# Seven products for the third group's first layer, and decays of keys and states moved from GpSimd to ScalarE

## The chip, the cores and the metric

The kernel runs on one core of a Trainium2 chip. The metric is the device time of one launch in microseconds. TensorE is called PE, VectorE DVE, ScalarE ACT, GpSimd POOL and SyncE SP, as in the profile.

## The reference

Decayed linear attention (4 batches, 8 heads, 768 positions, head size 64, in blocks) is followed by a two-layer network over all 3072 tokens:

```python
for b in range(nb):
    intra = np.einsum('bhic,bhjc->bhij', qb, kb) * Dmask[None]
    intra = np.einsum('bhij,bhjd->bhid', intra, vb)
    inter = np.einsum('bhid,bhde->bhie', qb * lam_pow[None], kv_state)
    out[:, :, sl] = intra + inter
    kb_dec = kb * rev_pow[None]
    kv_state = lam_block[None, :, None, None] * kv_state + np.einsum('bhsd,bhse->bhde', kb_dec, vb)
...
h = x @ w_in                      # 512 -> 2048
sp = np.where(h > 20.0, h, np.log1p(np.exp(np.minimum(h, 20.0))))
g = h * np.tanh(sp)
return (g @ w_out).astype(np.float32)   # 2048 -> 512
```

All decays are powers of one number per head. So within a group of positions a key is scaled by a factor that depends on its position and head, and a state by one factor per head.

## The kernel before, in words

The 768 positions are cut into six groups of 128; a group holds 512 tokens, 128 of each batch. The groups are numbered 0 to 5 in the code, so that "the third group" is `n = 2`. For each group and batch:

- `load_pair` (L84) issues the loads of keys, queries and values from POOL, two batches at a time, with a cast to 16 bits. Each kind has four buffers.
- Keys and queries are transposed ("turned") either by PE and a copy (`turn_pe`, L221) or by SP's transposing DMA (`turn_dma`, L239), which writes `kT` and `qT` for two batches.
- `decay_k` (L246) multiplies keys by `lk`, giving `kd`, on DVE or POOL.
- `scores` (L250) multiplies `kT` with `qT` on PE; DVE masks the two halves.
- `outputs` (L272) adds the part from the state `w` and the part from the masked scores on PE; DVE scales the result to `xn`, and SP's transposing DMA (or PE and ACT) writes it to `xt`, the network's input.
- `state` (L299) multiplies `kd` with the values on PE; DVE adds the old state (`raw`), and `raw` times the table `lbm` gives the new state `w`, on POOL mostly.

The network's first layer takes `xt` of a group to `hsg`. Done plainly it is 16 units of four 128x512 matmuls (`unit`, L337). Done "by seven products" (`set_step`, L419) it works on 2x2 blocks: four sets (`set_of`), each with seven products of four 128x256 matmuls where eight would be needed. This takes sums of the weights (`w_sum`, four for each of four sets) and of the input (`x_sums`, four per group), both on DVE, two copies per set on ACT (`seed` and `p5`) and two additions on DVE (L437, L441). The second layer (`dense2`, L529) works by seven products for all groups but the first; it is cut into 14 halves, which the code calls with `h()` between the other work.

The order is written out by hand: each engine executes its instructions in the order in which the code names them, and waits at each until its operands are there. In the part from L812 on, the loop over `n` runs a stage in which group `n` has its second layer, `n + 1` its first, and `m = n + 2` its attention. The table `KINDS` says for each stage whether the first layer is plain (`p`) or by seven products (`s`); stage 1, which has the third group's first layer, is plain. Ahead of the loop, the second group's first layer runs by pairs of units (`two_units`), with the third group's attention between them, and then the first group's plain second layer (`plain2`).

POOL has one queue as well. Loads, decays of keys and decays of states stand in it in the order of the code. A load waits for its buffer, and for the landing of the load eight places before it.

Of the kernel before, what the change touches and what calls it, by code (L numbers as in the profile page):

```python
# [20 lines left out]
def kernel(  # L21
# [12 lines left out]
    C = 128  # L34
# [165 lines left out]
    def state_decays():  # L200
        lbt = lb.rearrange("p (j t) -> p t j", t=2)
        for hp in range(2):
            rs = slice(64 * hp, 64 * hp + 64)
            nc.vector.tensor_copy(lbm[rs, :, rs], bc(lbt[rs, hp, :], 2, D))

# [40 lines left out]
    def decay_k(n, b, eng):  # L246
        kd[n, b] = work.tile([128, H, D], F16, name="kd", tag="kd", bufs=4)
        eng.tensor_tensor(out=kd[n, b], in0=kn[n, b], in1=bc(lk, 2, D), op=ALU.mult)

    def scores(n, b, tags="eo"):  # L250
        p_ = [bank(t, [JP, C]) for t in tags]
        for j in range(JP):
            for t in range(2):
                rs = slice(64 * t, 64 * t + 64)
                nc.tensor.matmul(p_[t][:, j, :], kT[n, b][rs, j, :], qT[n, b][rs, j, :],  # L255
                                 start=True, stop=True)
        for t in range(2):
            tag, bufs = ("sb", 4) if n > 0 or b < 2 else (f"xsum{b % 2 * 2 + t}", 1)
            sb[n, b, t] = work.tile([128, JP, C], F16, name="sb", tag=tag, bufs=bufs)
            nc.vector.tensor_tensor(out=sb[n, b, t], in0=p_[t], in1=dm[:, t], op=ALU.mult)  # L260

# [10 lines left out]
    def outputs(n, b, turn=None, tag="z"):  # L272
# [11 lines left out]
        nc.vector.tensor_tensor(out=xn, in0=po, in1=bc(lq, 2, D), op=ALU.mult)  # L284
        dst = x_tile(n)[:, :, b * C : (b + 1) * C]
# [13 lines left out]
    def state(n, b, tag, eng, later=False, home=("raw", 2)):  # L299
# [8 lines left out]
        else:  # L308
            raw = work.tile([128, JP, 128], F32, name="raw", tag=home[0], bufs=home[1])
            nc.vector.tensor_tensor(out=raw, in0=pv, in1=wst[n, b], op=ALU.add)  # L310
            wst[n + 1, b] = w_new
            decay = lambda: eng.tensor_tensor(out=w_new, in0=raw, in1=lbm, op=ALU.mult)  # L312
            return decay if later else decay()
        wst[n + 1, b] = w_new
# [320 lines left out]
    scores(0, 0)  # L635
    turn_pe(0, 1, first_banks)
# [10 lines left out]
    for b in range(B):  # L647
        decay_k(0, b, nc.vector)
# [12 lines left out]
    state(0, 0, "e", nc.vector)  # L661
    state(0, 1, "o", nc.vector)
    unit(0, 2, "A")
    unit(0, 3, "B")
    state(0, 2, "e", nc.vector)
    state(0, 3, "o", nc.vector)
# [18 lines left out]
    def out1(b, turn, po, pv):  # L685
        later[b] = outputs(1, b, turn, po)
        return state(1, b, pv, nc.vector if b < 2 else nc.gpsimd, b < 2,
                     ("raw", 2) if b < 2 else (("p5", "c22")[b - 2], 1))
# [6 lines left out]
    for t in "kqv":  # L695
        load_pair(t, 2, 1)
    mask_decays()
    first_units(9, 10, 11, 4, 5, 6)
    decay_k(1, 0, nc.vector)
    turn1(0, "Hz")  # L700
    first_units(7)
    turn1(1, "GC")
    scores(1, 0)
    decay_k(1, 1, nc.vector)
# [13 lines left out]
    decay_k(1, 2, nc.vector)  # L718
# [12 lines left out]
    two_units(1, 8, 0)  # L731
# [3 lines left out]
    decay_k(2, 0, nc.vector)  # L735
    decay_k(2, 1, nc.vector)
    w_sum(0, 0, nc.vector)
    w_sum(0, 1, nc.vector)
    two_units(1, 12, 0)
    turn_dma(2, 1)  # L740

# [3 lines left out]
    def attended(n, b):  # L745
        outputs(n, b)
        state(n, b, "H", nc.gpsimd)
# [4 lines left out]
    w_sum(0, 2, nc.vector)  # L752
    w_sum(0, 3, nc.vector)
# [6 lines left out]
    two_units(1, 6, 1)  # L760
    weight_sum(0, 1)
    two_units(1, 8, 1)
    attended(2, 1)
    for t, bp in (("k", 0), ("q", 0), ("v", 0)):
        load_pair(t, 3, bp)
# [5 lines left out]
    w_sum(2, 0, nc.vector)  # L771
    w_sum(2, 1, nc.vector)
    w_sum(2, 2, nc.vector)
    w_sum(2, 3, nc.vector)
# [9 lines left out]
    decay_k(2, 2, nc.vector)  # L784
# [4 lines left out]
    decay_k(2, 3, nc.vector)  # L789
    weight_sum(2, 0)  # L790
    plain2(1, 2, 3)
    plain2(2, 0)
    attended(2, 3)
    for t, bp in (("k", 1), ("q", 1), ("v", 1)):
        load_pair(t, 3, bp)
    sums(1, 0, 0, 1)
    plain2(2, 1, 2, 3)
    weight_sum(2, 1)
    plain2(3, 0, 1, 2, 3)
    sums(1, 0, 2, 3)  # L800
    busy(1)
# [10 lines left out]
    KINDS = {1: "pppp", 2: "ssss", 3: "ssss", 4: "ssss"}  # L812
    WSUMS = {(1, 0): (1,), (1, 1): (3,)}

    for n in range(1, NG - 1):
# [3 lines left out]
        def u(*units):  # L819
            for ni in units:  # L820
                unit(n + 1, ni, next_bank())

        held = []

        def s_(b):
            if m < NG:
                if b == 0 and not last:
                    decay_k(m, 0, nc.gpsimd)
                scores(m, b)
                release()  # L830

        def o_(b):
            if m < NG:
                outputs(m, b)
                if last:
                    return
                if b < B - 1:
                    decay_k(m, b + 1, nc.gpsimd)
                if "s" in KINDS[n]:
                    held.append(lambda: state(m, b, "z", nc.gpsimd))  # L840
                else:
                    state(m, b, "e", nc.gpsimd)
# [10 lines left out]
        def ws(n, i):  # L853
            for x in WSUMS.get((n, i), ()):
                for t in range(4):
                    w_sum(x, t, nc.vector)

        kinds = KINDS[n]
        sets = []
        for i, x in enumerate((0, 2, 1, 3)):  # L860
            spare = ("e", "z", "o") if m >= NG else ("A", "C", "B")
            alone = (("A", "B", "C"), spare)
            turn = i % 2 if kinds[i - 1] == "s" else 0
            sets.append(set_of(n + 1, x, alone[turn]) if kinds[i] == "s" else None)
# [10 lines left out]
        def opening(i):  # L875

            if kinds[i] == "s":
                mm(i, "m1")
                s_(i)
                mm(i, "seed")  # L880
                if i != 1:
                    settle()
            elif i == 0:
                s_(i)
# [42 lines left out]
        fresh = kinds[0] == "s" and KINDS[n - 1][3] == "p"  # L927
# [3 lines left out]
        if "s" in kinds:  # L931
            x_sums(n + 1, 0, 1, 2, 3)
        if not fresh:
            opening(0)
        if m < NG:
            turn_dma(m, 1)
        if kinds[0] == "s":
            h(1)
            if fresh:
                mm(0, "m2")  # L940
                h(1)
                mm(0, "m5", "m6")
            else:
                mm(0, "m2", "m5", "m6")
                sums(n, 1, 0, 1)
                h(1)
            o_(0)
            fetch(("k", 0), ("q", 0))
            if fresh:
                h(1)  # L950
            closing(0)
        else:
            u(0)
            sums(n, 1, 0, 1)
            if n == 1:
                weight_sum(3, 0)
                weight_sum(3, 1)
            h(1)
            u(1)
            h(1)  # L960
            u(2)
            o_(0)
            fetch(("k", 0), ("q", 0))
            u(3)
# [5 lines left out]
        if kinds[1] == "s":  # L970
            settle()
            mm(1, "m2")
            h(1)
            mm(1, "m5", "m6")
            sums(n, 1, 2)
            h(1)
            o_(1)
            fetch(("v", 0), ("k", 1))
            closing(1)
        else:  # L980
            u(8)
            settle()
            s_(1)
            sums(n, 1, 2, 3)
            ws(n, 0)
            h(1)
            u(9, 10)
            o_(1)
            fetch(("v", 0), ("k", 1))
            h(1)  # L990
            u(11)
# [3 lines left out]
        if kinds[1] == "s":  # L995
            sums(n, 1, 3)
# [3 lines left out]
        if kinds[2] == "s":  # L1000
            mm(2, "m2", "m5", "m6")
            o_(2)
            fetch(("q", 1), ("v", 1))
            h(1)
            closing(2)
            h(1)
            sums(n + 1, 0, 0, 1)
            h(1)
        else:
            u(4)  # L1010
            settle()
            s_(2)
            u(5)
            ws(n, 1)
            h(1)
            u(6)
            o_(2)
            fetch(("q", 1), ("v", 1))
            h(1)
            sums(n + 1, 0, 0, 1)  # L1020
            h(1)
            u(7)
# [3 lines left out]
        if kinds[3] == "s":  # L1026
            h(1)
            mm(3, "m2", "m5")
            h(1)
            mm(3, "m6")  # L1030
            o_(3)
            h(1)
            mm(3, "m7", "m3")
            owed.append(3)
            release()
            sums(n + 1, 0, 2, 3)
        else:
            s_(3)
            h(1)
            u(12)  # L1040
            settle()
            h(1)
            o_(3)
            u(13)
            sums(n + 1, 0, 2, 3)
            h(1)
            u(14)
        more = n + 1 < NG - 1
        if more:
            halves = dense2(n + 1)  # L1050
            h(1)
        if kinds[3] == "s":
            if more:
                h(1)
            settle()
        else:
            settle()
            u(15)
            if more:
                h(1)  # L1060
# [33 lines left out]
```

## Time and profile before

| | |
|---|---|
| median of 3 runs | 204.99 us (204.48 to 205.32) |
| the profiled execution | 204.73 us |
| its span, first to last instruction | 202.9 us |
| PE busy | 194.7 us, 96% |
| DVE busy | 148.0 us, 73% |
| ACT busy | 98.2 us, 48% |
| POOL busy | 81.8 us, 40% |
| mean granted clock of PE | 0.994 |

A row of a timeline has the start and the length in us, the engine, the line of the code, the operation and its tiles (out<-in), and in brackets the idle time ahead of it and what ended that. `x4` means that four instructions are merged; matmuls are pipelined, so one lasts longer than the time to the next. The rows of DMA queues have packets, megabytes and the time of those packets as a share of 16 engines; q0 carries the loads that POOL issues, q1 what SP issues.

### The profile page before, as it was taken

The page shows a single profiled execution, that of the slowest core. Times are in us where ns is not written, and L with a number is a line of the kernel's source. Part 1 is how long each engine was busy: PE and PEld are TensorE (multiplying, and loading weights), DVE is VectorE, ACT ScalarE, POOL GpSimd, SP SyncE. Part 2 cuts the span into 40 slices and gives each one's busy share as a digit, 9 for nine tenths or more (in the row PEclk, how much of TensorE's full clock was granted, in tenths as well). Part 3 has the DMA queues.
Part 4 walks back from the last instruction along what each step waited for, and adds up shares of the span by engine and source line. Part 5 has one row for each costly group of instructions (what it writes and reads, how often), then busy time and mean ns, then how long its engine had stood idle before and what let it go on. Part 6 is the DMA issues. An engine that isn't in the chain of part 4 may idle for free.

```text
span 202.9 us, 4669 instructions
## 1 busy us (share of the span) xinstructions
PE 194.7 (96%) x1931; PEld 150.1 (74%) x1931; DVE 148.0 (73%) x247; ACT 98.2 (48%) x176; POOL 81.8 (40%) x78
## 2 busy tenths in 40 slices
PE   7989999989999999999999999999999999999990
PEld 3867456878855556667668888988888988888890
DVE  6597558699978977689868698699588657179041
ACT  4685664658431124342264672456465384826300
POOL 7999452580292590848493377230000000000020
PEclk9999999999999999999999999999999999999997
DMA  9999999999999999999999999983213211003123
GB/s 131 134 142 198 175 180 156 157 204 201 148 142 153 223 164 175 178 109 117 176 218 172 126 79 158 189 193 89 29 26 81 79 53 53 0 3 119 43 100 105
DMA packets 109336, 26.26 MB, mean 129 GB/s; under 512 B 99458, under 2 KB 108802, under 8 KB 109314
## 3 DMA queue, kind: packets, MB, share of 16 engines
q0 software_dynamic: 77568, 13.37, 91.3%
q1 hardware_dynamic: 30704, 12.33, 29.2%
q10 hardware_dynamic: 1042, 0.26, 0.6%
q8 instruction: 15, 0.25, 0.5%
q14 instruction: 7, 0.06, 0.1%
HBM read 27.26 MB, written 6.29 MB: 165 GB/s over the span
## 4 chain that ended last, share of the span: by engine, by line
PE 77%; DMA 9%; POOL 7%; ACT 2%; DVE 2%; issue 1%; POOLq 0%; DVEq 0%; ACTq 0%
PE bG L523 15%; PE bH L523 13%; DMA vn<-in_v_dram 8%; PE bB L412 6%; PE bC L412 5%; PE bA L412 4%; PE bA L329 3%; PE be L255 3%; PE bB L329 3%; PE bA L355 2%; PE bC L355 2%; PE bB L355 2%; POOL win L96 2%; PE bC L329 2%; PE bz L281 2%; PE bA L574 2%
## 5 line engine op out<-in xcount | busy, mean ns | idle before, releaser
L312 POOL TENSOR_TENSOR w<-raw,lbm 128x512 f16<-128x512 f32 x14 | 20.4, 1458 | 41.9 <-DVE raw L310 41.8
L523 PEld LDWEIGHTS <-gsum 128*128 128x128 f16 x336 | 31.2, 98 | 4.2
L523 PEld LDWEIGHTS <-hsg 128*128 128x128 f16 x240 | 23.0, 98 | 4.4
L605 POOL TENSOR_TENSOR c<-p,u 128x512 f32<-128x512 f32 x1 | 1.3, 1276 | 58.7 <-DVE p L604 58.7
L260 DVE TENSOR_TENSOR sb<-be,dm 128x512 f16<-128x512 f32 x22 | 15.1, 687 | 8.4 <-PE bo L255 8.4
L523 PE MATMUL bH<-tsum,gsum 128*128 128x256 f16 x160 | 20.4, 273 | 0.0
L329 PEld LDWEIGHTS <-win 128*128 128x128 f16 x136 | 12.6, 98 | 10.3 <-DMA win<-in_moe_w_in_dram 0.5
L412 PEld LDWEIGHTS <-wsum 128*128 128x128 f16 x192 | 18.5, 98 | 2.2
L523 PE MATMUL bG<-wout,hsg 128*128 128x256 f16 x160 | 19.9, 273 | 0.0
L486 DVE TENSOR_TENSOR gsum<-hsg 128x1024 f16<-128x1024 f16 x20 | 15.6, 784 | 1.6 <-ACT hsg L335 1.6
L412 PEld LDWEIGHTS <-win 128*128 128x128 f16 x144 | 13.8, 98 | 2.2 <-issue 0.5
L260 DVE TENSOR_TENSOR sb<-bo,dm 128x512 f16<-128x512 f32 x22 | 15.0, 680 | 0.0
L284 DVE TENSOR_TENSOR xn<-bz,lq 128x512 f16<-128x512 f32 x18 | 12.3, 685 | 2.9 <-PE bz L281 2.9
L355 PEld LDWEIGHTS <-win 128*128 128x128 f16 x128 | 12.0, 98 | 1.6
L87 POOL DMA_DIRECT2D kn<-in_k_dram x10 | 11.9, 1190 | 2.8 <-PE bB L329 1.5
L87 POOL DMA_DIRECT2D qn<-in_q_dram x10 | 11.8, 1179 | 1.7 <-PE bA L329 0.9
L87 POOL DMA_DIRECT2D vn<-in_v_dram x10 | 11.7, 1172 | 1.4 <-DMA win<-in_moe_w_in_dram 1.2
L416 ACT ACTIVATE hsg<-bC 128x512 f16<-128x512 f32 x10 | 5.9, 594 | 13.0 <-PE bC L412 13.0
L412 PE MATMUL bA<-xt,win 128*128 128x256 f16 x80 | 12.0, 272 | 0.1
L329 PE MATMUL bA<-xt,win 128*128 128x512 f16 x44 | 11.3, 380 | 0.0
L574 PEld LDWEIGHTS <-hsg 128*128 128x128 f16 x64 | 6.0, 98 | 6.9
L335 ACT ACTIVATE hsg<-bA 128x512 f16<-128x512 f32 x11 | 6.6, 597 | 8.6 <-PE bA L329 8.6
(189 smaller groups left out, 445.4 us busy)
## 6 DMA issues: line engine op xcount, KB each, us to landing
out_dram<-osum SPq DMA_DIRECT2D x23, 256.0 KB, 3.2
kn<-in_k_dram POOLq DMA_DIRECT2D x10, 256.0 KB, 8.7
qn<-in_q_dram POOLq DMA_DIRECT2D x10, 256.0 KB, 8.0
vn<-in_v_dram POOLq DMA_DIRECT2D x10, 256.0 KB, 9.7
wout<-in_moe_w_out_dram POOLq DMA_DIRECT2D x4, 512.0 KB, 15.2
win<-in_moe_w_in_dram POOLq DMA_DIRECT2D x3, 512.0 KB, 10.5
vz<-in_v_dram POOLq DMA_DIRECT2D x2, 256.0 KB, 6.5
kn<-in_k_dram POOLq DMA_DIRECT2D x3, 128.0 KB, 4.6
```

The source lines that it names most:

```text
L87: nc.gpsimd.dma_start(out=tile_, in_=rows(src, n, 2 * bp, 2))
L255: nc.tensor.matmul(p_[t][:, j, :], kT[n, b][rs, j, :], qT[n, b][rs, j, :], start=True, stop=True)
L260: nc.vector.tensor_tensor(out=sb[n, b, t], in0=p_[t], in1=dm[:, t], op=ALU.mult)
L284: nc.vector.tensor_tensor(out=xn, in0=po, in1=bc(lq, 2, D), op=ALU.mult)
L312: decay = lambda: eng.tensor_tensor(out=w_new, in0=raw, in1=lbm, op=ALU.mult)
L329: nc.tensor.matmul(open_[n, ni][:, lo:hi], win[ni // 4][:, kc, (ni % 4) * 128 : (ni % 4) * 128 + 128], xt[n][:, kc, lo:hi], start=(opens a ...
L335: nc.scalar.activation(h_tile(n)[:, ni, :], open_.pop((n, ni)), AF.Mish)
L355: nc.tensor.matmul(t[:, u, :], win[ni // 4][:, kc, m : m + 128], xt[n][:, kc, cs], start=(u == 0 and kc == 0), stop=(kc == NKC - 1), skip_ ...
L412: nc.tensor.matmul(t[:, u, :], lhs, rhs, start=(fresh and u == 0 and kk == 0), stop=(kk == 1), skip_group_check=True)
L486: nc.vector.tensor_tensor(out=gsum[n, i][:, ks, :], in0=a, in1=b, op=op)
L523: nc.tensor.matmul(t, lhs(kk, blk), rhs(kk)[:, lo:hi], start=(fresh and kk == 0), stop=(kk == HK - 1), skip_group_check=True)
L574: nc.tensor.matmul(po, hsg[n][:, ki, b * C : (b + 1) * C], wout[part][:, kk, :], start=(ki == 0), stop=(ki == NKI - 1))
```

## The change

The third group's first layer is done by seven products as the later ones are: stage 1 takes the branch that stages 2 to 4 took, and the code for plain stages is removed. It needs the weight sums earlier. Those of sets 0 and 2 now stand in the first group, that of set 1 in the second group's first layer, that of set 3 before its end, and the last sums of the second layer's weights before stage 1.

Keys of the third group's second pair and of the later groups are decayed by ACT, one head of two batches at a time (`decay_heads`, 128x128 each). States are added on DVE in two pieces, only the blocks that count, into two lasting tiles `raws` that are zeroed once, and are decayed by ACT with a scale per pair of heads, four instructions for a state (`decay` in `state`). POOL keeps two state decays of the second group. In the second group, the fourth batch's keys are decayed earlier, and the third batch's `xn` comes between the two halves of the fourth batch's score mask. The loads of the fourth group's second pair are named with the first pair's.

```diff
+    def decay_heads(m, pair=None):
+        if pair:
+            decayed_pair(*pair)
+            heads_left.extend(pair + (h,) for h in range(H))
+        for _ in range(min(m, len(heads_left))):
+            n, bp, h = heads_left.pop(0)
+            src, dst = pairs["k", n, bp], decayed[n, bp]
+            nc.scalar.activation(dst[:, h : 2 * H : H, :], src[:, h : 2 * H : H, :], AF.Copy,
+                                 scale=lk[:, h : h + 1])
...
-            nc.vector.tensor_tensor(out=raw, in0=pv, in1=wst[n, b], op=ALU.add)
-            wst[n + 1, b] = w_new
-            decay = lambda: eng.tensor_tensor(out=w_new, in0=raw, in1=lbm, op=ALU.mult)
-            return decay if later else decay()
+        raw = raws[b % 2]
+        for rs in (slice(0, 64), slice(64, 128)):
+            nc.vector.tensor_tensor(out=raw[rs, :, rs], in0=pv[rs, :, rs],
+                                    in1=wst[n, b][rs, :, rs], op=ALU.add)
+
+        def decay():
+            for j in range(JP):
+                nc.scalar.activation(w_new[:, j, :], raw[:, j, :], AF.Copy,
+                                     scale=lbp[:, j : j + 1])
+
+        return decay
...
     scores(1, 2)
+    decay_k(1, 3)
     two_units(1, 2, 0)
     two_units(1, 4, 0)
-    scores(1, 3)
-    out1(2, "G", "z", "H")
-    decay_k(1, 3, nc.vector)
+    mask3 = scores(1, 3, apart=True)
+    out1(2, "G", "z", "H", mask3)
     two_units(1, 6, 0)
     later[2]()
-    out1(3, "G", "e", "o")
     for decay in decays1:
         decay()
+    out1(3, "G", "e", "o")
...
     attended(2, 1)
-    for t, bp in (("k", 0), ("q", 0), ("v", 0)):
-        load_pair(t, 3, bp)
+    for bp in range(2):
+        for t in "kqv":
+            load_pair(t, 3, bp)
...
-    KINDS = {1: "pppp", 2: "ssss", 3: "ssss", 4: "ssss"}
-    WSUMS = {(1, 0): (1,), (1, 1): (3,)}
+    decays = []
...
+        def scaled(i):
+            while decays:
+                decays.pop(0)()
+            if i < 2:
+                if not last:
+                    decay_heads(H // 2, (m, 1) if i == 0 else None)
+            elif m + 1 < NG - 1:
+                decay_heads(H // 2, (m + 1, 0) if i == 2 else None)
...
+            mm(1, "m5")
+            scaled(1)
+            mm(1, "m6")
```

POOL's queue after the loads of the third group's second pair (`kn_461` and its two neighbours; numbers tell buffers apart, L87 are loads, L312 state decays, L248 key decays), before:

```order
L87 DMA kn_461<-in_k_dram 128x16x64
L87 DMA qn_463<-in_q_dram 128x16x64
L87 DMA vn_465<-in_v_dram 128x16x64
L312 TENSOR_TENSOR w2_436<-raw_757,lbm_134 128x512
L312 TENSOR_TENSOR w3_443<-raw_798,lbm_134 128x512
L312 TENSOR_TENSOR w0_410<-raw_943,lbm_134 128x512
L312 TENSOR_TENSOR w1_417<-raw_1013,lbm_134 128x512
L87 DMA kn_1016<-in_k_dram 128x16x64
L87 DMA qn_1018<-in_q_dram 128x16x64
L87 DMA vn_1020<-in_v_dram 128x16x64
L312 TENSOR_TENSOR w2_436<-raw_1124,lbm_134 128x512
L312 TENSOR_TENSOR w3_443<-raw_1185,lbm_134 128x512
```

The same place of POOL's queue in the changed kernel (L348 is the state decay that is left):

```order
L87 DMA kn_466<-in_k_dram 128x16x64
L87 DMA qn_468<-in_q_dram 128x16x64
L87 DMA vn_470<-in_v_dram 128x16x64
L348 TENSOR_TENSOR w2_441<-raw_770,lbm_134 128x512
L348 TENSOR_TENSOR w3_448<-raw_817,lbm_134 128x512
L87 DMA kn_1034<-in_k_dram 128x16x64
L87 DMA qn_1036<-in_q_dram 128x16x64
L87 DMA vn_1038<-in_v_dram 128x16x64
L87 DMA kn_1040<-in_k_dram 128x16x64
L87 DMA qn_1042<-in_q_dram 128x16x64
L87 DMA vn_1044<-in_v_dram 128x16x64
L87 DMA kn_1397<-in_k_dram 128x16x64
```

The decays of the third group's states (`w0_410<-raw_943` and on) no longer stand ahead of the fourth group's loads; its six loads and the fifth group's follow directly.

ACT's queue in the changed kernel, in the second set of the third group's first layer (L480 is the copy `p5`, L357 the state decays, L270 the key decays, L462 the activation, L472 the copy `seed`):

```order
L480 ACTIVATE p5_1472<-bB_1467 128x512
L357 ACTIVATE w0_415<-raw_152,lbp_154 128x128 x4
L270 ACTIVATE kd_1370<-kn_1040,lk_149 128x2x64 x4
L462 ACTIVATE hsg_1350<-bB_1467 128x2x256
L472 ACTIVATE bB_1554<-bA_1528 128x512
L462 ACTIVATE hsg_1350<-c22_1521 128x2x256
```

Eight small activations now stand between `p5` and the activation of the set's third result.

DVE's queue around the third and fourth batch of the second group in the changed kernel (L258 keys, L284 score masks, L313 `xn`, L347 and L352 states):

```order
L258 TENSOR_TENSOR kd_688<-kn_119,lk_149 128x512
L284 TENSOR_TENSOR sb_746<-be_736,dm_148 128x512
L313 TENSOR_TENSOR xn_761<-bz_748,lq_150 128x512
L284 TENSOR_TENSOR sb_763<-bo_737,dm_148 128x512
L347 TENSOR_TENSOR raw_770<-bH_765,w2_441 128x512
L313 TENSOR_TENSOR xn_810<-be_797,lq_150 128x512
```

Before, both masks stood ahead of the first `xn`, and this `kd` between the first `raw` and the second `xn`.

More of the change, by code (lines that the diff above doesn't have):

```diff
@@ L244, in turn_dma, with decayed_pair, decay_k, scores @@
                 to[n, 2 * bp + i] = tile_[:, i * JP : (i + 1) * JP, :]
[L246 to L250, printed above, removed]
+    decayed = {}
+    def decayed_pair(n, bp):
+        t = work.tile([128, 2 * H, D], F16, name="kd", tag="kd", bufs=2)
+        decayed[n, bp] = t
+        for i in range(2):
+            kd[n, 2 * bp + i] = t[:, i * H : (i + 1) * H, :]
+    def decay_k(n, b):
+        if b % 2 == 0:
+            decayed_pair(n, b // 2)
+        nc.vector.tensor_tensor(out=kd[n, b], in0=kn[n, b], in1=bc(lk, 2, D), op=ALU.mult)
+    heads_left = []
+    def decay_heads(m, pair=None):
[7 more added lines that the diff above has]
+                                 scale=lk[:, h : h + 1])
+    def scores(n, b, tags="eo", apart=False):
         p_ = [bank(t, [JP, C]) for t in tags]
@@ L256, in scores, with mask @@
                                  start=True, stop=True)
-        for t in range(2):
+        def mask(t):
             tag, bufs = ("sb", 4) if n > 0 or b < 2 else (f"xsum{b % 2 * 2 + t}", 1)
@@ L260, in scores @@
             nc.vector.tensor_tensor(out=sb[n, b, t], in0=p_[t], in1=dm[:, t], op=ALU.mult)
+        mask(0)
+        if apart:
+            return lambda: mask(1)
+        mask(1)
     def first_outputs(b, tag):
@@ L297, in outputs, with state @@
         return later
-    def state(n, b, tag, eng, later=False, home=("raw", 2)):
+    raws = [work.tile([128, JP, 128], F32, name="raw", tag="raw", bufs=2) for _ in range(2)]
+    lbp = const.tile([128, JP], F32, name="lbp")
+    def state(n, b, tag, home=None):
         pv = bank(tag, [JP, 128])
@@ L635 @@
     scores(0, 0)
+    for t in raws:
+        nc.vector.memset(t, 0.0)
     turn_pe(0, 1, first_banks)
@@ L683, in turn1, with out1 @@
         turn_pe(1, b, banks, "q", eng)
[L685 to L688, printed above, removed]
+    def out1(b, turn, po, pv, then=None):
+        later[b] = outputs(1, b, turn, po, then)
+        return state(1, b, pv, ("p5", "c22")[b - 2] if b > 1 else None)
     first_units(8)
@@ L817 @@
         last = m >= NG - 1
-        def u(*units):
-            for ni in units:
-                unit(n + 1, ni, next_bank())
         held = []
         def s_(b):
[L826 to L830, printed above, removed]
-        def o_(b):
[L833 to L842, printed above, removed]
+            scores(m, b)
+            release()
+        def o_(b):
+            outputs(m, b)
+            if not last:
+                held.append(lambda: decays.append(state(m, b, "z")))
+        def scaled(i):
+            while decays:
+                decays.pop(0)()
+            if i < 2:
+                if not last:
+                    decay_heads(H // 2, (m, 1) if i == 0 else None)
+            elif m + 1 < NG - 1:
+                decay_heads(H // 2, (m + 1, 0) if i == 2 else None)
         def release():
@@ L861 @@
             spare = ("e", "z", "o") if m >= NG else ("A", "C", "B")
-            alone = (("A", "B", "C"), spare)
-            turn = i % 2 if kinds[i - 1] == "s" else 0
-            sets.append(set_of(n + 1, x, alone[turn]) if kinds[i] == "s" else None)
+            sets.append(set_of(n + 1, x, (("A", "B", "C"), spare)[i % 2]))
         owed = []
@@ L999 @@
             turn_dma(m + 1, 0)
[L1000 to L1022, printed above, removed]
-        opening(3)
[L1026 to L1060, printed above, removed]
+        mm(2, "m2", "m5")
+        scaled(2)
+        mm(2, "m6")
+        o_(2)
+        fetch(("q", 1), ("v", 1))
+        h(1)
+        closing(2)
+        h(1)
+        sums(n + 1, 0, 0, 1)
+        h(1)
+        opening(3)
+        h(1)
+        mm(3, "m2", "m5")
+        scaled(3)
+        h(1)
+        mm(3, "m6")
+        o_(3)
+        h(1)
+        mm(3, "m7", "m3")
+        owed.append(3)
+        release()
+        sums(n + 1, 0, 2, 3)
+        halves = dense2(n + 1)
+        h(2)
+        settle()
     sums(NG - 1, 1, 2, 0, 1, 3)
```

167 lines of the change are left out of this document (74 added, 93 removed).

## Prediction

> **What bounds the kernel now.** I read the page's head first, then the engines' busy time in stretches, then the timelines of single engines around the places that the change touches.
>
> ```profile
> span 202.9 us, 4669 instructions
> PE 194.7 (96%) x1931; PEld 150.1 (74%) x1931; DVE 148.0 (73%) x247; ACT 98.2 (48%) x176; POOL 81.8 (40%) x78
> ```
>
> The reader should see one engine, TensorE (PE), at 96%. That is an average, so the stretches come next: the stage that holds the third group's first layer (73.30 to 105.57), and the one after it, which has seven products already.
>
> ```profile
> 73.30:105.57 32.27, 32.27 (x290) 22.06 (x288) 24.43 (x40) 12.52 (x21) 20.06 (x17) 1.00 1.81 159
> 105.57:134.55 28.98, 28.98 (x323) 25.21 (x320) 24.08 (x39) 14.53 (x27) 14.46 (x13) 1.00 1.41 153
> ```
>
> The columns are length, then busy time of PE, weight loads, DVE, ACT and POOL. PE is busy for the whole of both at full clock. So a matmul less there is time gained, and work added to VectorE (DVE) or ScalarE (ACT) costs nothing until it makes PE wait. The only waits of PE between 32 and 134 us stand here, in its timeline:
>
> ```profile
> 41.80 0.40 PE L293 MATMUL bG<-ident,xn 128*128 128x128 f16 x4 [0.32 <-DVE xn L284]
> ...
> 42.99 0.40 PE L302 MATMUL bo<-vn,kd 128*128 128x128 f16 x4 [0.34 <-DVE kd L248]
> ```
>
> **The matmuls.** 64 matmuls of 128x512 go, 112 of 128x256 come (16 units of four; 4 sets of seven products of four). Their spacing, from the same timeline:
>
> ```profile
> 84.43 1.03 PE L329 MATMUL bC<-xt,win 128*128 128x512 f16 x4
> 85.29 1.03 PE L329 MATMUL bA<-xt,win 128*128 128x512 f16 x4
> ...
> 110.89 0.60 PE L412 MATMUL bB<-xsum,wsum 128*128 128x256 f16 x4
> 111.33 0.60 PE L412 MATMUL bC<-xt,wsum 128*128 128x256 f16 x4
> 111.76 0.60 PE L412 MATMUL bA<-xt,win 128*128 128x256 f16 x4
> ```
>
> Four of 512 take 85.29 - 84.43 = 0.86 us; four of 256 take (111.76 - 110.89)/2 = 0.435. So 16 x 0.86 = 13.76 becomes 28 x 0.435 = 12.18: **1.58 us less**. A check: the first stretch holds 16 eighths-of-a-second-layer, the second 14, each eight matmuls of 256 (0.87); 32.27 - 28.98 - 2 x 0.87 = 1.55.
>
> What pays for it: the extra input sums and the eight extra combining adds go to DVE, whose load becomes about that of the second stretch (24.08 of 28.98, under which PE lost nothing), and weight sums go earlier. Nothing on the path.
>
> **The stall at 41 to 43 us.** The change computes the fourth batch's decayed keys earlier, and puts DVE's `xn` ahead of the second half of the score mask. Each of the two waits above is shorter than the one DVE operation taken out from in front of it, so I take both as gone: **0.66 us less**. Bounds: 0, if the eight new ACT decays queued there delay the next group's `qT` as long; and 0.66.
>
> **ACT's small decays.** 8 per pair of batches for keys and 4 per state are added, none of which the trace shows. Nearest rows: a 128x8 with a scale read from memory, and the 128x512 around the place where the decays will sit, behind `p`:
>
> ```profile
> 11.85 0.30 ACT L191 ACTIVATE lk<-lnb,ek 128x8 f32<-128x8 f32 x1
> 12.04 0.30 ACT L191 ACTIVATE lq<-lnb,eq 128x8 f32<-128x8 f32 x1
> ...
> 108.84 0.60 ACT L545 ACTIVATE osum<-bG 128x512 f32<-128x512 f32 x1 [0.28 <-PE bG L523]
> 109.36 0.60 ACT L434 ACTIVATE p<-bC 128x512 f32<-128x512 f32 x1
> 111.96 0.60 ACT L416 ACTIVATE hsg<-bC 128x512 f16<-128x512 f32 x1 [2.01 <-PE bC L412]
> ```
>
> Spacing 0.19 at 8 elements and 0.52 at 512 bound one of 128 elements; in proportion it is 0.19 + 0.33 x 120/504 = 0.27, which I take. The largest batch, eight, is 2.2 us, against an idle 2.01 in that very place. A spill of 0.2 us delays the activations behind it, and PE only where a bank comes free late. I cost it at nothing. Without cover (0.52 each, 4.2 us) five such places would lose up to 2 us each.
> [...]
>
> **GpSimd's queue (POOL), which I take to decide.** POOL issues every load, in order, between its own multiplications:
>
> ```profile
> 42.42 3.44 POOL L312 TENSOR_TENSOR w<-raw,lbm 128x512 f16<-128x512 f32 x2 [0.16 <-DVE raw L310]
> 52.04 1.27 POOL L312 TENSOR_TENSOR w<-raw,lbm 128x512 f16<-128x512 f32 x1 [6.18 <-DVE raw L310]
> 55.78 1.65 POOL L312 TENSOR_TENSOR w<-raw,lbm 128x512 f16<-128x512 f32 x1 [2.47 <-DVE raw L310]
> 57.37 1.21 POOL L87 DMA_DIRECT2D kn<-in_k_dram  x1
> ```
>
> The fourth group's loads start at 57.37 only because POOL sat behind the states at 52.04 and 55.78. Those two multiplications leave POOL. Its row after the pair at 42.42 is now the load, so loads start near 45.9 us, 11.5 us sooner, and six stand in one run, with the fifth group's behind. POOL's freed time is worth nothing in itself; what it triggers is. At that moment SP turns the third group's second pair (`kT`, `qT`) by DMA:
>
> ```profile
> SPq L242 <- DMA kn<-in_k_dram: 55.5, 2, 53.1
> ```
> ```profile
> 54.33 1.32 SPq L242 DMA_TRANSPOSE kT<-kn  x1
> 55.77 1.25 SPq L242 DMA_TRANSPOSE qT<-qn  x1
> ```
>
> SP waited for the load of `kn` until 54.33. That load is in the opening stream and does not move with PE, so these turns keep their start. Time from issue to landing, from the DMA view around each `qT` turn: first this one, then those issued at 66.84, 91.72, 105.43 and 121.00, each with loads under way:
>
> ```profile
> qT<-qn SPq DMA_TRANSPOSE x1, 3.4
> ```
> ```profile
> qT<-qn SPq DMA_TRANSPOSE x1, 4.5
> ```
> ```profile
> qT<-qn SPq DMA_TRANSPOSE x1, 7.6
> ```
> ```profile
> qT<-qn SPq DMA_TRANSPOSE x1, 6.4
> ```
> ```profile
> qT<-qn SPq DMA_TRANSPOSE x1, 6.7
> ```
>
> So it landed at 55.77 + 3.4 = 59.2, in a gap without loads. In the changed kernel there is no gap. The four others have a median of 6.5: 62.3. A second route is the packets by queue, from 57.7 to 59.2 (turns alone) and from 95.5 to 97.7 (q0 loads, q1 turns):
>
> ```profile
> q1 hardware_dynamic: 1184, 0.29, 101.5%
> ```
> ```profile
> q0 software_dynamic: 1083, 0.14, 104.5%
> q1 hardware_dynamic: 713, 0.18, 75.2%
> ```
>
> Turns go at 1184/1.5 = 789 packets per us alone, at 713/2.2 = 324 beside loads. A pair is 0.26 MB at 250 bytes, about 1,024 packets; two are 2.6 us alone, 6.3 beside loads, 3.7 more: 62.9. Bounds 59.2 (no effect) and 55.77 + 7.6 = 63.4; I take 62.3. PE needs it here:
>
> ```profile
> 57.06 3.62 PE L574 MATMUL bG<-wout,hsg 128*128 128x512 f16 x16
> 60.61 0.23 PE L255 MATMUL be<-qT,kT 64*128 64x128 f16 x1
> ```
>
> Without the stall PE arrives at 60.61 - 0.66 = 59.95 and waits 62.3 - 59.95 = **2.35 us more**. Behind this score matmul stands all of PE's queue. Since the wait ends at a landing, any other delay before 60 us of up to 2.35 (weight sums on DVE while POOL issues loads, the ACT decays at 43) costs nothing.
>
> [...]
>
> **Sum**, on the profiled execution's own 204.73 (span 202.9 and 1.83 around it): 204.73 - 1.58 - 0.66 + 2.35 = **204.8**. The runs' median is 204.99, 0.26 above that execution and inside their spread, so I don't shift it. Half a percent, what a measurement here can tell from no change, is 1.02 us: 203.97 to 206.01.
>
> **Rivals.**
> 1. *No collision*: loads issued earlier land earlier and leave the turns alone, or PE reaches the scores no sooner than `qT`. Then only the gains stay: 204.73 - 1.58 - 0.66 = 202.5. For it: each load's bytes are the same, the opening stream is in order. Against it: the four loaded landings above, none as short as 3.4. Chance 0.30.
> 2. *The collision repeats, slower than before.* SP's turns are one queue: behind the late pair stand four `xt` turns, half as long, and the fourth group's pair, in all 6 x 1,024 packets from about 55.5 on. The first product that reads an input sum, which needs all of `xt`, comes 3.1 us after its set opens, as these rows of the later stage show:
>
> ```profile
> 105.57 0.60 PE L412 MATMUL bA<-xt,win 128*128 128x256 f16 x4
> ...
> 108.67 0.60 PE L412 MATMUL bC<-xsum,wsum 128*128 128x256 f16 x4
> ```
>
>    In the third group that is 73.3 + 1.74 for two halves + 1.69 of shift + 3.1 = 79.8. It decides once turns fall below 6144/(79.8 - 55.5) = 253 packets per us: with `qT` at 63.4 (3.45 of waiting) and 1.5 us more at 79.8, 204.73 - 2.24 + 3.45 + 1.5 = 207.4. For it: loads now stand eight deep. Against: at 324 per us the turns end at 55.5 + 19.0 = 74.5, with only two stores between them. Chance 0.22.
> 3. *ACT becomes the limit*: its decays cost 0.4 or more, so that banks come free late in five sets, some 0.8 us each: 204.8 + 4 = 208.8. For it: only 2 us idle behind `p`. Against: the spacing of the rows above. Chance 0.06.
>
> **How the numbers follow.** The forecast, one wait of 1.3 to 3.4 us for `qT`, has 0.42 and by itself gives 203.7 to 205.9. Rival 1 lies wholly under 203.97 and the forecast's lower end adds a little: faster 0.33. Most of the forecast and none of the others: same 0.40. Rivals 2 and 3 with a rest: slower 0.27. Range 202.4 to 207.4, from rival 1 to rival 2; the likeliest case's own is 203.7 to 205.9.
>
> **What would show it.** Four matmuls of L412's kind where L329's stood in the third group, and no PE wait near 41 to 43. POOL's first load behind the pair of multiplications near 46 us. `kT` and `qT` turns issued near 54.3 and 55.8, landing after 61, and PE idle before its score matmuls near 60 us, released by that DMA. Four or eight ACT decays behind each `p`, 0.25 to 0.3 us apart. It is wrong if `qT` still lands by 60, or if PE's idle time is elsewhere; it is too low if PE also waits between 75 and 80.

## The result, and the profile after

The changed kernel takes 210.76 us (median, 210.47 to 211.19) against 204.62 us (204.17 to 205.32) of the kernel before: a ratio of 1.0292, 95% interval 1.0269 to 1.0316. It is slower by 2.9%, where the forecast was 204.8 us with a range up to 207.4. The profiled execution took 211.19 us, 6.46 more than that of before. Its page's head and clock row:

```profile
span 209.4 us, 4881 instructions
PE 195.0 (93%) x1979; PEld 154.8 (74%) x1979; DVE 149.0 (71%) x273; ACT 128.4 (61%) x280; POOL 54.3 (26%) x58
...
PEclk9999999999995899999999999999999999999999
```

PE is as busy as before (194.7), though it has less to multiply, and for two of the 40 slices, from 63 us, it does not run at full clock. Its timeline there:

```profile
56.44 3.62 PE L620 MATMUL bG<-wout,hsg 128*128 128x512 f16 x16
63.92 0.26 PE L278 MATMUL be<-qT,kT 64*128 64x128 f16 x1 [3.87 <-DMA qT<-qn]
64.46 3.60 PE L620 MATMUL bA<-wout,hsg 128*128 128x512 f16 x8
...
69.81 1.90 PE L620 MATMUL bA<-wout,hsg 128*128 128x512 f16 x8
```

The wait for `qT` is where it was forecast, but it is 3.87 us instead of 2.35. Behind it eight matmuls take 3.60 us; the next eight of the same kind take 1.90 from 69.81 on. The granted clock in three stretches of one microsecond (the number behind POOL's; columns as in the prediction):

```profile
62.00:63.00 1.00, 0.00 (x0) 0.00 (x0) 0.00 (x0) 0.00 (x0) 0.00 (x0) 0.96 1.64 157
63.00:64.00 1.00, 0.08 (x3) 0.08 (x4) 0.00 (x0) 0.00 (x0) 0.28 (x1) 0.50 2.41 153
...
69.00:70.00 1.00, 1.00 (x13) 0.53 (x11) 0.99 (x3) 0.00 (x0) 0.49 (x1) 0.62 2.33 148
```

PE falls idle at 60.05 (63.92 - 3.87). A mean of 0.96 is 0.08 us at half clock, so the clock halves at 62.92; a mean of 0.62 is 0.76 us, so it is whole again at 69.76. Now the two queues, POOL's (which issues the loads) and SP's (the turns), and the DMA view's line for `qT`:

```profile
44.79 1.21 POOL L87 DMA_DIRECT2D kn<-in_k_dram  x1
...
53.74 1.15 POOL L87 DMA_DIRECT2D qn<-in_q_dram  x1 [4.19 <-DMA kn<-in_k_dram]
```
```profile
53.46 1.34 SPq L243 DMA_TRANSPOSE kT<-kn  x1
55.10 3.46 SPq L243 DMA_TRANSPOSE qT<-qn  x1
```
```profile
qT<-qn SPq DMA_TRANSPOSE x1, 8.8
```

The loads do run ahead, from 44.79 instead of 57.37, and the turn issued at 55.10 lands at 63.9.

The rest of the loss stands in the stages after it. Stretches from the first product of the second group's second layer to that of the fourth group's, before and after:

```profile
73.32:132.37 59.05, 59.05 (x590) 45.31 (x589) 46.35 (x75) 26.30 (x47) 33.36 (x28) 1.00 1.66 157
```
```profile
79.35:139.21 59.86, 58.50 (x638) 50.35 (x637) 45.92 (x81) 46.02 (x114) 6.86 (x6) 1.00 1.25 138
```

These hold the third group's seven products and should be 1.58 shorter; they are 0.81 longer, with 1.36 us in which PE is idle. So the profiled executions differ like this, as far as the start of the fourth group's second layer (139.21 against 132.37, 6.84 later):

| stretch of PE | before | after | difference | forecast |
|---|---|---|---|---|
| up to the arrival at the third group's third scores | 60.61 | 60.05 | -0.56 | -0.66 |
| wait for `qT` there | 0 | 3.87 | +3.87 | +2.35 |
| from those scores to the second group's second layer | 12.71 | 15.43 | +2.72 | 0 |
| from there to the fourth group's second layer | 59.05 | 59.86 | +0.81 | -1.58 |

Against the forecast's sum (204.84) the profiled execution is 6.35 us too long: 0.10, 1.52, 2.72 and 2.39 in these four rows, less 0.38 that it gains after them.

### The profile page after: what moved, and what is told of

It is laid out like the page before. It is cut to its first block, busy times and chain, and to the rows that moved or that the text cites. A ratio compares the mean times of both kernels' runs of the same rounds, so it can differ in the third digit from the quotient of the medians.

```text
span 209.4 us, 4881 instructions
## 1 busy us (share of the span) xinstructions
PE 195.0 (93%) x1979; PEld 154.8 (74%) x1979; DVE 149.0 (71%) x273; ACT 128.4 (61%) x280; POOL 54.3 (26%) x58
## 4 chain that ended last, share of the span: by engine, by line
PE 69%; DMA 14%; DVE 6%; POOL 4%; ACT 3%; issue 1%; SPq 1%; POOLq 0%; DVEq 0%; ACTq 0%
PE bH L569 13%; PE bG L569 10%; PE bB L458 7%; DMA xt<-xn 6%; PE bC L458 5%; DMA qT<-qn 4%; PE bA L458 4%; DMA win<-in_moe_w_in_dram 3%; PE be L278 3%; PE bA L620 3%; PE bB L375 2%; PE bA L375 2%; PE bB L401 2%; PE bz L305 2%; PE bA L401 2%; PE bz L310 2%
## 5 line engine op out<-in xcount | busy, mean ns | idle before, releaser
L458 PEld LDWEIGHTS <-wsum 128*128 128x128 f16 x256 | 24.8, 98 | 3.6 <-issue 0.8
L569 PEld LDWEIGHTS <-hsg 128*128 128x128 f16 x240 | 22.8, 98 | 3.2
L284 DVE TENSOR_TENSOR sb<-be,dm 128x512 f16<-128x512 f32 x22 | 15.2, 690 | 13.0 <-PE bo L278 12.8
L458 PEld LDWEIGHTS <-win 128*128 128x128 f16 x192 | 18.4, 98 | 2.9 <-issue 0.7
L87 POOL DMA_DIRECT2D vn<-in_v_dram x10 | 11.6, 1156 | 31.1 <-PE bz L336 22.4
L357 ACT ACTIVATE w<-raw,lbp 128x128 f16<-128x128 f32 x56 | 17.6, 395 | 0.0
L458 PE MATMUL bA<-xt,win 128*128 128x256 f16 x112 | 16.8, 272 | 0.2
L313 DVE TENSOR_TENSOR xn<-bz,lq 128x512 f16<-128x512 f32 x18 | 12.3, 685 | 4.5 <-PE bz L310 3.9
L284 DVE TENSOR_TENSOR sb<-bo,dm 128x512 f16<-128x512 f32 x22 | 15.0, 681 | 0.0
L462 ACT ACTIVATE hsg<-bC 128x512 f16<-128x512 f32 x14 | 8.3, 592 | 10.4 <-PE bC L458 10.4
L87 POOL DMA_DIRECT2D kn<-in_k_dram x10 | 11.7, 1173 | 10.1 <-DMA kT<-kn 5.1
L87 POOL DMA_DIRECT2D qn<-in_q_dram x10 | 11.7, 1168 | 9.6 <-DMA kn<-in_k_dram 7.4
L278 PE MATMUL be<-qT,kT 64*128 64x128 f16 x88 | 9.0, 226 | 5.4 <-DMA qT<-qn 4.2
L278 PEld LDWEIGHTS <-kT 64*128 64x128 f16 x192 | 6.0, 97 | 10.1 <-issue 6.8
L458 PE MATMUL bB<-xsum,wsum 128*128 128x256 f16 x88 | 13.2, 272 | 0.2 <-DVE bC L483 0.2
L401 PEld LDWEIGHTS <-win 128*128 128x128 f16 x128 | 12.0, 98 | 1.5
L270 ACT ACTIVATE kd<-kn,lk 128x128 f16<-128x128 f16 x40 | 12.5, 390 | 0.0
```

Source lines behind the costliest of these rows:

```text
L87: nc.gpsimd.dma_start(out=tile_, in_=rows(src, n, 2 * bp, 2))
L270: nc.scalar.activation(dst[:, h : 2 * H : H, :], src[:, h : 2 * H : H, :], AF.Copy, scale=lk[:, h : h + 1])
L357: nc.scalar.activation(w_new[:, j, :], raw[:, j, :], AF.Copy, scale=lbp[:, j : j + 1])
L401: nc.tensor.matmul(t[:, u, :], win[ni // 4][:, kc, m : m + 128], xt[n][:, kc, cs], start=(u == 0 and kc == 0), stop=(kc == NKC - 1), skip_ ...
L458: nc.tensor.matmul(t[:, u, :], lhs, rhs, start=(fresh and u == 0 and kk == 0), stop=(kk == 1), skip_group_check=True)
L462: nc.scalar.activation(h_tile(o.n)[:, 4 * o.s + 2 * r : 4 * o.s + 2 * r + 2, t * HC : t * HC + HC], src, AF.Mish)
```

## The experiments

Theory A: the loads that run ahead delay the turns; the wait and the slow clock follow from that. Theory B: ScalarE's 96 small decays cost the time. Two more came with the runs, C (the seven products bring waits of their own) and A2 (GpSimd's multiplications slow VectorE). Each run is given by its time, the ratio to the kernel before on the same chip, and PE's start at two places of its timeline: the third group's third scores ("scores"; before, 60.61) and the second group's second layer ("layer"; before, 73.32).

**Loads held back by two state decays on GpSimd.** The changed kernel with:

```diff
-        decays2.append(state(n, b, "H"))
+        decay = state(n, b, "H")
+        if b < 2:
+            nc.gpsimd.tensor_tensor(out=wst[n + 1, b], in0=raws[b], in1=lbm, op=ALU.mult)
+        else:
+            decays2.append(decay)
...
-    decays2.pop()()
...
-    decays2.pop()()
```

> The changed kernel, with the first two state decays of the third group on GpSimd as before (ScalarE no longer does them), so that the fourth group's loads again stand behind them. Theory A (loads that run ahead delay the DMA turns of the third group's second pair, PE waits 3.9 us for qT, and PE's clock then halves for another 2.7 us): loads start near 57 us, qT lands by 60, no wait before the scores, granted clock 1.00 there, 210.8 - 3.9 - 2.7 = 204.2 us. Theory B (the loads are innocent; ScalarE's small decays cost the 6 us): only 8 of 96 small decays go, 210 to 211 us.

208.85 us, 1.0203 (1.0181 to 1.0224); scores 60.22, layer 72.93. Loads start at 57.50, `qT` is there in time, the clock stays whole up to there and the first 73 us are 0.4 shorter than before. That much is as theory A has it. But the time is 4.65 above its 204.2: by the fourth group's second layer PE is 4.1 late (136.50 against 132.37), and most of the 4.5 us lost since go here:

```profile
109.95 0.61 PE L458 MATMUL bC<-xsum,wsum 128*128 128x256 f16 x4 [1.82 <-DVE xsum L436]
```
```profile
109.47 0.43 DVE L436 TENSOR_TENSOR xsum<-xt 128x512 f16<-128x512 f16 x1 [3.70 <-DMA xt<-xn]
```
```profile
110.00:112.00 2.00, 2.00 (x14) 1.59 (x15) 1.97 (x5) 1.40 (x5) 0.00 (x0) 0.71 1.64 154
112.00:114.00 2.00, 2.00 (x19) 1.65 (x18) 1.97 (x4) 2.00 (x7) 0.00 (x0) 0.50 1.67 155
```

Behind the two state decays nothing holds the loads: nine are issued in one run from 57.50. The last `xt` turn of the fourth group, issued at 102.54, lands 6.9 us later (before: issued at 101.06, landed 5.5 us later); its input sums, and with them PE, wait for it. The clock halves here too, at 110.84 (0.71 is 1.16 us of two at half), though PE was idle for only 1.82 us and had been back at work for 0.9. Holding the loads once moved the wait to a later landing. In the run with the 128x8 multiplications below, which holds them all along, PE does not wait there.

**The pair turned by PE instead of SP's DMA.** The changed kernel with:

```diff
-    turn_dma(2, 1)
+    turn_pe(2, 2, ("H", "z"))
     two_units(1, 12, 1)
+    turn_pe(2, 3, ("H", "z"))
```

> The changed kernel, with the third group's second pair turned by PE and copied by ScalarE and VectorE's place untouched, instead of SP's transposing DMA; the loads still run ahead. Theory A: the wait for qT and the slow clock behind it go, 16 transposes of 0.055 us come: 210.8 - 6.6 + 0.9 = 205.1 us. Theory B: four 0.5 us copies more on ScalarE, so 211 or more.

206.85 us, 1.0098 (1.0072 to 1.0123); scores 62.20, layer 74.91, clock 1.00 throughout. The wait and the slow clock go though the loads still run ahead: 3.9 us of the 6.1 come back. 1.75 us more than expected stay; PE still waits 0.85 for a later `qT` and 0.69 for the bank that the new transposes share with a state.

**Only the loads moved, in the kernel before.**

```diff
+    for bp in range(2):
+        for t in "kqv":
+            load_pair(t, 3, bp)
     attended(2, 0)
```
(and taken out at their old places)

> The kernel before, with nothing changed but the place of the fourth group's six loads in GpSimd's queue: ahead of the third group's state decays, as the changed kernel has them in effect. Theory A: qT lands near 63.5 instead of 59.2, PE waits about 3 us there and runs slow behind it for 2.7: 204.6 + 3 + 2.7 = 210.3 us. Theory B: 204.6 us, since loads are innocent and ScalarE has none of the small decays.

211.71 us, 1.0342 (1.0317 to 1.0367); scores 65.26 after a wait of 4.36 for `qT`, layer 80.67. No product, no decay and no engine of the work is changed, and 7 us are lost, somewhat more than in the changed kernel. Theory B falls as the main cause. The wait in PE's timeline:

```profile
65.26 0.26 PE L255 MATMUL be<-qT,kT 64*128 64x128 f16 x1 [4.36 <-DMA qT<-qn]
```

**One pair early.** The same with the first pair's three loads only.

> The kernel before, with three of the fourth group's loads (keys, queries and values of the first pair) ahead of the third group's state decays instead of six. Theory A, by bytes in flight: six early loads delayed qT from 59.2 to 65.3; three issue near 46 to 49 us and hold 0.79 MB moved at about 157 GB/s, 5 us of traffic behind what is still queued, so they are mostly landed when the turns are issued at 54 to 56: qT by 61 to 62.5, a wait of 0.5 to 2 us, no or a short fall of the clock, 205 to 207 us. If any early load has the whole effect, 211 us.

211.64 us, 1.0342 (1.0306 to 1.0378); scores 65.74 after 5.33 us, layer 81.28.

```profile
65.74 0.26 PE L255 MATMUL be<-qT,kT 64*128 64x128 f16 x1 [5.33 <-DMA qT<-qn]
```

My count of bytes was wrong: three loads do as much as six. The packets by queue in the changed kernel suggest why, from 55.1 to 57 and from 58 to 59 (q0 loads, q1 turns):

```profile
q0 software_dynamic: 2341, 0.30, 245.3%
```
```profile
q0 software_dynamic: 421, 0.05, 81.1%
q1 hardware_dynamic: 413, 0.11, 79.7%
```

The turns issued from 53.46 on move nothing up to 57 and 25 packets up to 58; then both queues move alike, 421 to 413. In the run with one pair early nothing moves up to 58 either. In the kernel before the turns are issued at 54.33, and between 55 and 56 they already move:

```profile
q0 software_dynamic: 517, 0.07, 102.5%
q1 hardware_dynamic: 246, 0.06, 29.8%
```

When the `qT` turn is issued, one load is under way in the kernel before (issued and not yet landed), four in the run with one pair early, six in the changed kernel and in the run with all six early. If loads queued at 54 us take the turns' first 4 us, the loads behind them matter less, and three do what six do; that is argued and not shown. No run here tells what delays their first packets.

**Matmuls of zeros in the wait**, first in the changed kernel (16, ahead of `attend(2, 2)`), then in the kernel before with one pair early (20):

```diff
     plain2(0, 0, 1, 2, 3)
+    busy(16)
     attend(2, 2)
```

> The changed kernel, with 16 matmuls of zeros (128x512, 0.22 us each, 3.5 us) ahead of the third group's third scores, in the time in which PE waits for qT. Theory A with the clock falling because PE idles: the wait stays, filled, the clock stays at 1.00, and 210.8 - 2.7 = 208.1 us. If PE's matmuls behind the wait are slow for another reason (memory contention, the loads themselves), 210.8 us.

210.69 us, 1.0293 (1.0271 to 1.0315); scores 63.91, layer 76.73, 2.6 earlier than in the changed kernel, at a clock of 1.00. But the time is that of the changed kernel, as the second expectation has it, though not for its reason: PE, now sooner, waits 1.03 for the next `qT` and 1.47 for the fourth group's input sums. VectorE's first such sum, in the changed kernel and here:

```profile
112.82 0.42 DVE L436 TENSOR_TENSOR xsum<-xt 128x512 f16<-128x512 f16 x1 [1.41 <-DMA xt<-xn]
```
```profile
112.80 0.42 DVE L436 TENSOR_TENSOR xsum<-xt 128x512 f16<-128x512 f16 x1 [3.35 <-DMA xt<-xn]
```

The `xt` turn lands at the same time in both, and PE's product starts at 113.61 and 113.28. So the clock was worth next to nothing there; a landing stood behind it. The changed kernel's own executions say the same: the mean clock was 0.984 in four of the six, 0.989 in one and 1.000 in one, and that one took 211.07 us.

> The kernel before with three early loads (as in the run with one pair early, 211.6 us), and with 20 matmuls of zeros (0.22 us each, 4.4 us) ahead of the third group's third scores, in the time in which PE waits 5.3 us for qT. If PE's idling is what halves its clock, the clock stays at 1.00 and the 2.7 us or more lost behind the wait come back, since in this kernel no later landing takes their place: 208.3 to 208.9 us. If the matmuls behind the wait are slow because of the transfers, 211.6 us.

209.92 us, 1.0266 (1.0236 to 1.0295), 1.7 under the run without the zeros and 1.0 above the upper end of the expectation; scores 65.85, layer 78.57. From scores to layer it takes 12.72 us as before, where the run without zeros took 15.54. The clock from 66 us, without and with them:

```profile
66.00:68.00 2.00, 2.00 (x13) 0.71 (x8) 1.64 (x3) 0.00 (x0) 0.00 (x0) 0.50 0.22 76
```
```profile
66.00:68.00 2.00, 2.00 (x18) 0.95 (x14) 1.73 (x3) 0.00 (x0) 0.00 (x0) 1.00 0.40 134
```

So here it is PE's idling that halves the clock (0.50 without the zeros, 1.00 with them), not the traffic: 2.8 us in these two executions, 1.7 in the medians. The profiled execution without zeros has the lowest mean clock of its four (0.978, the others 0.982 to 0.992) and is the longest of them, 212.69 us.

**The seven products alone.** The kernel before with `KINDS[1]` set to "ssss", the weight sums and the order at 41 to 43 us as in the changed kernel, and all decays left on GpSimd and VectorE.

> The kernel before, with the seven products in the third group's first layer, the weight sums moved as in the changed kernel and the reordering that removes the stall at 41 to 43 us; all decays of keys and states stay on GpSimd and VectorE, so the loads stay paced as before. Theory A (only the decays' move off GpSimd hurts, by what it does to the loads): 204.7 - 1.58 - 0.66 = 202.4 us. Theory C (the seven products in this stage bring their own waits, on VectorE's input sums and on banks): the small waits of the changed kernel's stages 1 and 2, 2.4 us, appear here too, 204.5 to 205 us.

205.58 us, 1.0053 (1.0026 to 1.0081); layer 72.42, 0.90 earlier, and then the gain is gone. The miss is 3.2 us against theory A, and theory C's kind of wait is there, 0.6 above its 205. The first wait for input sums, and VectorE and GpSimd ahead of the next stage's:

```profile
79.01 0.60 PE L420 MATMUL bC<-xsum,wsum 128*128 128x256 f16 x4 [1.62 <-DVE xsum L398]
```
```profile
104.18 1.76 DVE L494 TENSOR_TENSOR gsum<-hsg,gsum 128x1024 f16<-128x1024 f16 x1
105.94 1.19 DVE L398 TENSOR_TENSOR xsum<-xt 128x512 f16<-128x512 f16 x1
107.16 1.15 DVE L398 TENSOR_TENSOR xsum<-xt,xsum 128x512 f16<-128x512 f16 x1
108.23 0.41 DVE L398 TENSOR_TENSOR xsum<-xt 128x512 f16<-128x512 f16 x1
```
```profile
103.75 1.65 POOL L320 TENSOR_TENSOR w<-raw,lbm 128x512 f16<-128x512 f32 x1 [3.56 <-DVE raw L318]
105.35 2.67 POOL L248 TENSOR_TENSOR kd<-kn,lk 128x512 f16<-128x512 f16 x2
```

Sums that take 0.41 us otherwise take 1.2 beside GpSimd's multiplications; the second of the two slow ones ends 0.29 us after the two multiplications from 105.35 on (108.31 and 108.02). That overlap is not the whole account: ahead of the wait at 79.01 two sums take 1.53 us while the profile shows only loads being issued on GpSimd, behind a large multiplication.

```profile
70.22 1.53 DVE L494 TENSOR_TENSOR gsum<-hsg 128x1024 f16<-128x1024 f16 x1
```

**ScalarE's decays, with the loads paced.** The changed kernel, with GpSimd doing its old multiplications as well, into a tile that nobody reads (`pace_k` for the keys), and the loads at their old places:

```diff
+        if n > 1:
+            paced.append(lambda: nc.gpsimd.tensor_tensor(out=spare_tile, in0=raw, in1=lbm, op=ALU.mult))
...
+                pace_k(m, b + 1)
```

> The changed kernel with all of ScalarE's small decays, while GpSimd in addition does the multiplications it did before, at the old places, into a spare tile that nobody reads, and with the loads at their old places in its queue. Theory A: the loads are paced as before, qT lands by 60, no long wait, 202.5 us; what this is above the run with the seven products alone is the price of ScalarE's small decays. Theory B (ScalarE's decays cost the time): 206 us or more.

206.50 us, 1.0085 (1.0063 to 1.0107); layer 73.17, no long wait, clock 1.00. Taken by itself the time is theory B's (206 or more), and theory A's 202.5 is missed by 4. But the seven products alone, without any of these decays, take 205.58. So 0.9 is about what ScalarE's small decays cost (the two intervals overlap), and theory B falls as the account of the rest.

**The same with multiplications of 128x8**, so that loads wait for the same things and GpSimd does next to nothing:

```diff
-nc.gpsimd.tensor_tensor(out=spare_tile, in0=raw, in1=lbm, op=ALU.mult)
+nc.gpsimd.tensor_tensor(out=spare_tile[:, 0, 0:8], in0=raw[:, 0, 0:8], in1=lbm[:, 0, 0:8], op=ALU.mult)
```

> The changed kernel with the loads at their old places in GpSimd's queue and, in place of each of its old multiplications, one of 128x8 elements with the same operands' first columns, so that loads wait for the same things and GpSimd does almost nothing. Theory A2 (the loads must be held back, and GpSimd's large multiplications slow VectorE's 16-bit sums from 0.69 to 1.5 us beside them, which eats the seven products' gain): VectorE's sums take 0.69 and 0.42 us wherever GpSimd is not issuing loads, the waits for input sums shrink, 206.5 - 1 to 2 = 204.5 to 205.5 us. Theory A alone (GpSimd's own work is harmless): 206.5 us, as in the run with the full multiplications. Theory B (ScalarE's decays): 206.5 us too, or more.

203.98 us, 0.9967 (0.9951 to 0.9983); layer 73.00. That is 2.5 us less than with the full multiplications, 0.5 below theory A2's range, 6.8 less than the changed kernel, and 0.3% less than the kernel before. One group of VectorE's sums, with the full ones and with the small ones:

```profile
L543 DVE TENSOR_TENSOR gsum<-hsg,gsum 128x1024 f16<-128x1024 f16 x10 | 9.0, 901 | 0.2
```
```profile
L543 DVE TENSOR_TENSOR gsum<-hsg,gsum 128x1024 f16<-128x1024 f16 x10 | 6.9, 687 | 0.2
```

This pair of runs has the same ScalarE work, the same places of the loads and the same products; only the size of GpSimd's operations differs, and with it the time at which the loads are issued (the row at 70.38 stands at 68.94). The sums at the place of the 1.53 us above take 0.69 here, beside the same loads:

```profile
70.19 0.69 DVE L543 TENSOR_TENSOR gsum<-hsg 128x1024 f16<-128x1024 f16 x1
```

Why loads behind a large multiplication go with slow sums and loads behind a small one don't stays open.

**And with ScalarE's first eight decays later** (those of the second group's first two states, moved behind `turn_pe(2, 0, ...)`):

> As the run with the 128x8 multiplications, and ScalarE's eight decays of the second group's first two states moved behind its copies of kT and qT of the third group's first batch. If these eight (2.5 us in front of the copies) cause the 0.83 us wait at 47 us, it goes: 0.8 us less than that run. If the wait only moves (to the outputs that read the new states), nothing changes.

203.99 us, 0.9975 (0.9954 to 0.9997): no difference in the medians. The 0.83 us wait at 47 us goes, and one of 0.51 for a bank comes at 48.30. Its stretch between the two second layers:

```profile
72.78:131.32 58.54, 57.97 (x638) 50.17 (x636) 46.38 (x82) 45.81 (x114) 17.24 (x26) 1.00 1.58 158
```

0.51 us less than before: PE is busy 1.08 us less and idle for 0.57. This execution was the fastest of its 12 (203.33). The one profiled with the decays at their first place was the slowest of its 12 (204.75), and the same stretch takes 59.74 there, 0.69 more than before, most of it a wait for a turn:

```profile
88.72 0.21 PE L285 MATMUL be<-qT,kT 64*128 64x128 f16 x1 [1.14 <-DMA qT<-qn]
```

Both runs have the same median, so 0.51 is an upper end and not the usual gain.

## Why the prediction was wrong

- **The matmuls (-1.58): the size was right, and the step "Nothing on the path" fell.** Counted from start to start, the first-layer matmuls of the stretch between the two second layers take 26.3 us before and 24.8 in the last run (203.99 us), 1.54 less. Short stops take about 1.0 of that back, most of it behind the scores and the outputs; the two longest end with a result of VectorE. 0.57 shows as idle time; the rest hides in busy time, since a 128x256 matmul lasts 0.27 in the profile and the next one starts after 0.11. So that execution keeps 0.51, the one with the wait at 88.72 nothing, and with GpSimd at its old work nothing is left either (205.58 us). I argued from VectorE's mean load in a later stage (24.08 of 28.98). What counts is the opening of a stage, where token sums, masks and input sums stand in one row on VectorE while GpSimd multiplies. The trace of before had this too:

```profile
102.14 1.76 DVE L486 TENSOR_TENSOR gsum<-hsg,gsum 128x1024 f16<-128x1024 f16 x1
```

- **The stall at 41 to 43 us (-0.66): the two waits went, the gain did not come, and that the arrival fits is luck.** My lower bound came true: ScalarE's eight decays stand in front of `qT`. The scores of the second group's third batch and of the third group's first, before and after:

```profile
37.24 0.23 PE L255 MATMUL be<-qT,kT 64*128 64x128 f16 x1
47.48 0.23 PE L255 MATMUL be<-qT,kT 64*128 64x128 f16 x1
```
```profile
36.71 0.23 PE L278 MATMUL be<-qT,kT 64*128 64x128 f16 x1
46.86 0.21 PE L278 MATMUL be<-qT,kT 64*128 64x128 f16 x1 [0.83 <-ACT qT L238]
```
```profile
41.95 2.44 ACT L357 ACTIVATE w<-raw,lbp 128x128 f16<-128x128 f32 x8
```

  Between them lie 10.24 us before and 10.15 after; in the run with the seven products alone, where these decays are not on ScalarE, 9.25. PE arrives at 60.05, 0.1 from the forecast of 59.95, because it was 0.53 ahead by 36.71 already. 0.33 of that is a wait for a load at 31.85, which the run with one pair early, with the same code up to there, does not have.
- **ScalarE's small decays (0): right in price, wrong in that they cost nothing.** In ScalarE's timeline of the changed kernel:

```profile
86.11 1.26 ACT L270 ACTIVATE kd<-kn,lk 128x128 f16<-128x128 f16 x4
```

  At 0.39 for one (their mean in the page) four stand (1.26 - 0.39)/3 = 0.29 apart; I took 0.27. But the eight at 41.95 are on PE's path, with 0.83 us, and the run with paced loads puts the price of all of them at some 0.9 us. Moving these eight did not help, since a wait of 0.51 for a bank came in their place. Rival 3, 4 us in five sets, did not come.
- **GpSimd's queue: the mechanism was right, its place and time too (loads from 44.79, forecast 45.9). The term "2.35 us more" was mis-sized.** It measured 3.87, since the turn landed 8.8 us after its issue, beyond the bound of 7.6. I took landings from later turns, at whose issue one or two loads were under way; here there were six. In the changed kernel the turns moved next to nothing for 4 us (25 packets by 58 us, after an issue at 53.46). Neither of my two routes had that time; the second had a rate instead, 324 packets per us, where the trace then shows 413.
- **The step that was missing: what a wait of this length costs behind itself.** The forecast has a wait that ends, and full speed and timely landings after it. In this execution the clock is half from 62.92 to 69.76 us, and 2.72 us are lost. Without the halving they go to later landings instead, as the run with zeros shows (the execution at a clock of 1.000 was no shorter either), so the landings alone suffice for the loss. The kernel before gave no example on its path, its longest wait in that part being 0.34 us; only at its end, with PE idle from 198.2 on, does its clock halve, at 200.48. Half clock lasted 6.84 us here, behind a wait of 3.87, and 3.4 us in the run with the loads held back, where 1.82 us of idling came before it.
- **Rival 2 (the collision repeats) was half right.** Not at 79.8 us, where PE waited 0.27 in the changed kernel, but at the fourth group's input sums: 1.82 and 1.47 us in the two kernels whose first wait was taken away or filled. In the changed kernel itself PE came there too late to wait.

So the 6.1 us are the loads': moved early by themselves they cost 7.0 us, and a kernel that differs from the changed one by small operations in GpSimd's queue and by the place of three loads is 6.8 us faster. The steps that failed are the landing time (2.35 us taken, 3.87 measured), the path behind that wait, which was taken as free of further cost (2.72), and the path of the seven products, which was taken as free of waits (their 1.58 us did not show). The single terms do not add up across kernels, because a landing behind each of them takes over. What keeps the turns from moving for their first 4 us stays open.

## What to carry to other kernels

Work on a queue that also issues transfers is a clock for those transfers: without it the loads went from 57.37 to 44.79 us here. Before taking it away, ask what will hold them, and if need be leave a tiny operation that waits for the same thing. Price a long wait of PE with the slow clock behind it (half clock followed one of 1.82 us here, and none followed one of 1.47), and then look for the landing that stands behind. Read VectorE's load at the place where its results are awaited, and beside what GpSimd does there (a sum took 1.19 instead of 0.41 us), not as a mean over a stage.

## What was not expected of the hardware

- Transposing DMAs issued while loads are queued moved nothing for about 4 us (25 packets by 58 us after an issue at 53.46), and then as much as the loads, 413 against 421 packets per us. In the kernel before, with one or two loads under way, they moved 246 packets between 55 and 56 us after an issue at 54.33.
- The clock halved 2.9 us after the start of an idle time of 3.87 us, and 2.7 us after the start of one of 1.82, when PE was already at work again. It stayed halved for 6.84 and 3.4 us. Idle times of 1.47 and 1.14 us had no such effect in two other runs, whose executions had mean clocks of 0.995 and 0.996 (0.994 in the kernel before).
- VectorE's sums of 16-bit operands took 1.76 instead of 0.69 us, and 1.19 instead of 0.41, beside GpSimd's multiplications. While GpSimd did only small operations and issued loads, they took 0.69; behind a large multiplication, two took 1.53 beside loads alone.
